# Logits of four of twelve token tiles by VectorE instead of TensorE, and a lighter sum of squares

## The chip, the cores and the metric

One core of one Trainium2 chip runs the whole program. The metric is device time in microseconds of one execution. TensorE's granted clock has two levels here, 2.4 GHz (written 1.00 in the profile) and 1.2 GHz (0.50).

## The reference, cut to what matters

Three layers follow one another on 1536 tokens (2 batches of 768) with 512 features:

```
attention: 16 heads, local window 96 and 8 global keys, softmax, times v     -> x
gated MLP: xn = x / sqrt(mean(x*x) + 1e-6) * rms_g
           x = (silu(xn @ w_gate) * (xn @ w_val)) @ w_out                    -> x
experts:   skip = x @ w_skip;  logits = x @ w_gate  (8 experts)
           tokens with skip > 0: e = argmax(logits), g = softmax(logits)[e]
           out = x + g * (relu(x @ w1[e]) @ w2[e]);  the others: out = x
```

## The kernel before, in words

The order of the work is written out by hand: each engine executes its instructions in the order in which the program issues them, and a wait of one instruction holds up everything behind it on the same engine.

**Attention** runs over 24 items (8 pairs of heads times 3 thirds of the sequence) in a pipeline of five steps, with `t` counting the turns. `Rms.take` leaves the square of each finished third in an `sq` tile, four of them to a batch. `Rms.add` (POOL, L422) adds one `sq` tile of 128x768 onto the first, at `t` = 3 pr + 8 for two head pairs of each batch, so that two tiles are left. `Rms.stats` then sums over the partitions by TensorE (L444): for each of 6 blocks of 128 tokens, one product per `sq` tile with a 128-column matrix of ones as moving operand; each fp32 product is two instructions in the trace. In its last call (`g == 3`) VectorE makes `rv` = mean + 1e-6 (L448). `Rms.root` takes the inverse square root in small VectorE steps. For batch 0 these are handed out one by one between VectorE's attention operations of later turns by `tick()`; for batch 1 they run in one go after the loop.

**The gated MLP** is two products. Every fp32 product is made of three (high x high, high x low, low x high). In the second one, `gemm2`, token tile `t` (128 tokens, 0 to 11) takes 36 matmuls, three to each of 12 steps `k`. A dictionary of hooks puts other work behind steps 1, 5 and 9 of a tile; the program there is, for tile `t`:

- ahead of step 0: `ranks(t-2)` (two small TensorE products from `cum` and `oh`), then VectorE's `select(t-2)` and `gates(t-2)` (eight small operations, from `rp` L707 to the last `val` L693);
- behind step 1 (`one`): `turn(t-1)`, four TensorE transposes of `x2` (L580) and a ScalarE copy to `x2t` (L581); `split_h(t+1)`, six ScalarE casts `hh` (L567) and six VectorE subtractions `hl` (L568), without which tile `t+1` cannot start;
- behind step 5 (`two`): `logits(t-1)`, eight TensorE instructions of 9 columns (L589); `route(t-1)`, seven small VectorE operations from `rm` (L653) over `oh` (L663) to `cum`; `exps(t-1)`, one on VectorE (L674) and an exponential on ScalarE (L677); in some tiles `split_next`, which splits chunks of 128x1024 of the experts' weights: `ewh` by ScalarE (L845), `ewl` by VectorE (L854);
- behind step 9: `slots(t-2)`, one TensorE product (L720) that reads what `gates` and `select` wrote;
- at the end ScalarE writes `x2` of tile `t` (L608).

`logits` and `ranks` share a ring of two PSUM buffers (tag `ps1`).

**The experts** follow. Their weights come through SP's DMA queue into `Slots`, a list of 128x1024 buffers; at the start of `gemm2` it holds 8, and 8 loads are issued (`load_next(8)`).

Of the kernel before, what the change touches and what calls it, by code (L numbers as in the profile page):

```python
# [191 lines left out]
def attention(s, rms):  # L192
# [8 lines left out]
    es = []  # L201
# [133 lines left out]
    for t in range(n + 4):  # L335
        a, b, c, d, e = (items[t - z] if 0 <= t - z < n else None for z in range(5))
        if a:
            qk(a, t)
        if c:
            trans(c, 0)  # L340
            trans(c, 1)
        if d:
            pv(d, 0)
            pv(d, 1)
        if b:
            zadd(b)
            tick()
            zrec(b)
            tick()
            norm(b, 1, 1, nc.gpsimd if t < n else nc.vector)  # L350
            if t < n:
                norm(b, 1, 0, nc.gpsimd)
            norm(b, 0, 0, nc.vector)
            tick()
        if a:
            ttr(a, 0, 0)
            tick()
        if b:
            norm(b, 0, 1, nc.vector)
            tick()  # L360
        if a:
            ttr(a, 0, 1)
            tick()
            ttr(a, 1, 0)
            tick()
        if b and t >= n:
            norm(b, 1, 0, nc.vector)
            tick()
        if a:
            ttr(a, 1, 1)  # L370
            tick()
        if c:
            evac(c, 0, nc.vector)
        if e:
            out(e)
        for half in range(2):
            if a:
                exp(a, half)
        if c:
            evac(c, 1, nc.scalar)  # L380
        if a:
            pr, g = a
            if g == 1 and 2 < pr + 2 < 8:
                load(pr + 2)
            if g == 2 and 2 < pr + 2 < 8:
                loadv(pr + 2)
        for pr in range(8):
            if pr % 4 in (1, 2) and t == 3 * pr + 8:
                rms[pr // 4].add()
        yield t  # L390


class Rms:
# [30 lines left out]
    def general(self, xg):  # L424

        s, nc = self.s, self.s.nc
        for hp in range(4):
            x = s.rpool.tile([128, 768], F32, name="gx", bufs=1)
            r = 512 * self.b + 128 * hp
            nc.sync.dma_start(x, xg[r:r + 128, :])  # L430
            sq = self.sq[hp] if hp < 2 else s.rpool.tile([128, 768], F32, name="gsq", bufs=1)
            for g in range(3):
                c = slice(256 * g, 256 * g + 256)
                self.parts(hp, g, x[:, c], sq[:, c])
            if hp > 1:
                nc.vector.tensor_tensor(self.sq[1], self.sq[1], sq, ALU.add)

    def stats(self, g, psum=None):
        s, nc = self.s, self.s.nc
        if g == 0:  # L440
            self.ss = psum or s.spare
        for j in range(2 * g, min(2 * g + 2, 6)):
            for z, sq in enumerate(self.sq):
                nc.tensor.matmul(self.ss[:, j:j + 128], lhsT=sq[:, 128 * j:128 * j + 128], rhs=s.ones,  # L444
                                 start=z == 0, stop=z == len(self.sq) - 1)
        if g == 3:
            self.v = s.rpool.tile([128, 6], F32, name="rv", bufs=2)
            nc.vector.tensor_scalar(self.v, self.ss[:, 0:6], 1.0 / 512.0, 1e-6, ALU.mult, ALU.add)  # L448

    def root(self):  # L450

        s, nc, v = self.s, self.s.nc, self.v
        r = s.r[self.b] = s.cpool.tile([128, 6], F32, name=f"r{self.b}")
        nc.vector.tensor_scalar(r.bitcast(I32), v.bitcast(I32), 1, None, ALU.arith_shift_right)
        yield
        nc.vector.tensor_scalar(r.bitcast(I32), r.bitcast(I32), -1.0, float(0x5F3759DF), ALU.mult, ALU.add)
        yield
        t = s.rpool.tile([128, 6], F32, name="rt", bufs=2)
        for _ in range(3):
            nc.vector.tensor_tensor(t, r, r, ALU.mult)  # L460
            yield
            nc.vector.scalar_tensor_tensor(out=t, in0=t, scalar=-0.5, in1=v, op0=ALU.mult, op1=ALU.mult)
            yield
            nc.vector.scalar_tensor_tensor(out=r, in0=t, scalar=1.5, in1=r, op0=ALU.add, op1=ALU.mult)
            yield
        d = self.diag = s.rpool.tile([128, 6, 128], F32, name="rd", tag="sq", bufs=4)
        for j in range(6):
            if j < 3:
                nc.vector.tensor_scalar(d[:, j, :], s.ident, r[:, j:j + 1], None, ALU.mult)
                yield  # L470
            else:
                nc.scalar.activation(d[:, j, :], s.ident, AF.Copy, scale=r[:, j:j + 1])
# [111 lines left out]
def logits(s, t, ks=range(4)):  # L584

    if ks[0] == 0:
        s.lg[t] = s.ps_g.tile([128, 9], F32, name="lg", tag="ps1", bufs=2)
    for k in ks:
        s.nc.tensor.matmul(s.lg[t], lhsT=s.xt[t][:, k, :], rhs=s.w9t[:, k, :], start=k == 0, stop=k == 3)  # L589


def gemm2(s, t, hooks={}):
# [103 lines left out]
def ranks(s, t, pool=None, tag="ps1"):  # L696

    rk = s.rk[t] = (pool or s.ps_g).tile([128, 8], F32, name="rk", tag=tag, bufs=1 if pool else 2)
    s.nc.tensor.matmul(rk, lhsT=s.ones16, rhs=s.cum[:, t, :], start=True, stop=False)
    s.nc.tensor.matmul(rk, lhsT=s.tri, rhs=s.oh[:, t, :], start=False, stop=True)  # L700


def select(s, t):

    V = s.nc.vector
    c = (s.ixpool if t >= 9 else s.hpool).tile([128, 8], F32, name="rp", bufs=2)
    V.tensor_tensor(c, s.oh[:, t, :], s.rk[t], ALU.mult)  # L707
    yield
    V.tensor_reduce(s.pos[:, t:t + 1], c, AX.X, ALU.add)
    yield  # L710
    sel = s.sel[t] = (s.ixpool if t >= 9 else s.hpool).tile([128, 256], F32R, name="sel", bufs=3 if t >= 9 else 2)
    V.tensor_scalar(sel, s.slot, s.pos[:, t:t + 1], None, ALU.is_equal)
    yield
# [10 lines left out]
def run(*parts):  # L724

    parts = list(parts)
    while parts:
        parts = [p for p in parts if next(p, FAR) is None]
# [213 lines left out]
def attn_moe_kernel(ctx, tc, qx, kx, vx, rel, ints, wgv, w_out, rms_g, w9, w9t, w1, w2, out):  # L942
# [96 lines left out]
    for t in att:  # L1039
        if t < 3:  # L1040
            next(bias)
        if t == 4:
            load_unit(s, units[0])
            load_unit(s, units[1])
        if t >= 13:
            next(unit, None)
        if t == 16:
            with tc.If(flag == 0):
                rms[0].general(s.xg)
        if t == 17:  # L1050
            for g in range(4):
                rms[0].stats(g)
            s.small = rms[0].root()
        if 19 <= t < 22:
            run(s.small)
            rms[0].spread(t - 19)
        if t in (25, 26, 27):
            gemm1s()
        if t == 26:
            ss = s.ps_n.tile([128, 133], F32, name="ss", tag="rb", bufs=2)  # L1060
            rms[1].stats(0, ss)
            rms[1].stats(1)
        if t == 27:
            rms[1].stats(2)
    with tc.If(flag == 0):
        rms[1].general(s.xg)
        for g in range(3):
            rms[1].stats(g, ss)
    rms[1].stats(3)


    run(rms[1].root())
# [57 lines left out]
        halves += [(j + 1, 0)] * (j < 8) + [(j, 1)]  # L1130
    loads = iter([(j, 4 * half + c) for j, half in halves for c in range(4)])
    s.slots = Slots()
    s.slots.add(rawpool, [f"raw{z}" for z in range(8)])

    def load_next(n, eng=nc.sync):
        for _ in range(n):
            x = next(loads, None)
            if x:
                if x == (8, 0):
                    experts[8].e = nc.values_load(  # L1140
                        s.eji[0:1, 0:1], engines=[mybir.EngineType.SP], min_val=0, max_val=7,
                        skip_runtime_bounds_check_because="a minimum with 7 of a count")
                experts[x[0]].load(x[1], eng)
# [8 lines left out]
            if x:  # L1152
                experts[x[0]].split(x[1], nc.scalar, nc.vector)

    load_next(8)
    s.early = s.ixpool.tile([128, 512], F32, name="early", bufs=1)
    nc.gpsimd.memset(s.early, 0.0)

    def routed(t):
        logits(s, t)  # L1160
        run(route(s, t))
        exps(s, t)

    for t in range(11):
        if t >= 2:
            ranks(s, t - 2)
            run(select(s, t - 2))
        if t >= 2:
            run(gates(s, t - 2))

        def one():
            if t >= 1:
                turn(s, t - 1)
                split_h(s, t + 1)
            if t in (2, 6, 10):
                for q in range(6):
                    s.slots.add(early if t < 10 and q == 0 else big, [f"h{t // 4}{q}"])
                load_next({6: 0, 10: 6}.get(t, 0))

        def two():  # L1180
            if t >= 1:
                routed(t - 1)
            split_next({2: 3, 3: 2, 6: 2, 7: 1}.get(t, 0))
            load_next({7: 4}.get(t, 0))

        gemm2(s, t, {(0, 1): one, (0, 5): two, (0, 9): lambda: t >= 2 and slots(s, t - 2)})


    slt = s.ixpool.tile([24, 256], F32, name="slt", bufs=1)
# [241 lines left out]
```

## Time and profile before

| | |
|---|---|
| median of 3 runs | 554.51 us (551.69 to 555.45) |
| profiled execution | 554.08 us, its span 552.3 us |
| TensorE (PE) busy | 524.2 us, 95% of the span |
| VectorE (DVE) | 404.8 us, 73% |
| ScalarE (ACT) | 277.5 us, 50% |
| GpSimd (POOL) | 140.8 us, 25% |

Times in the rows are microseconds from the start of the span. Attention takes the first 97 us or so, the gated MLP runs to about 423 us (`gemm2` from 303), the experts to the end. In a timeline, a row gives start, length, engine, line, operation, tile written <- tiles read, shapes and count; a bracket gives the idle time of the engine before it and who ended it.

### The profile page before, as it was taken

To read this page: it belongs to the slowest core of one execution; us is meant where nothing else is said; L and a number is where in the kernel's file an instruction comes from. 1 tells how busy PE (TensorE), PEld (TensorE's weight loads), DVE (VectorE), ACT (ScalarE), POOL (GpSimd) and SP (SyncE) were. 2 spreads that over 40 slices of the span, in tenths; PEclk is the share of its full clock that TensorE was granted. 3 is DMA by queue.
4 is the path that set the end of the run, shared out by engine and by line. 5 is a ranking of instruction groups with operands and counts; after the bars stand their busy time and mean duration, and the time that the engine had idled before them with its cause. 6 is when DMAs were issued, how large, how long until landed. Compare 5 with 4: busy or idle time off the path is not lost. (4 is left out here: it accounts for less than half of the span.)

```text
span 552.3 us, 9096 instructions
## 1 busy us (share of the span) xinstructions
PE 524.2 (95%) x3132; PEld 425.8 (77%) x3132; DVE 404.8 (73%) x1026; ACT 277.5 (50%) x631; POOL 140.8 (25%) x140
## 2 busy tenths in 40 slices
PE   3899886999999999999999999999999999999994
PEld 2676665878888888888888888878789787888883
DVE  5899999567888688868884358456443599999971
ACT  2799896324332233333333255244231587988850
POOL 2446545001222212212220200000000512666001
PEclk9999998999999999999999999999999999999998
DMA  8653511112323323323313512116171599999300
GB/s 301 210 211 139 173 36 39 33 46 77 105 88 113 113 79 114 114 79 113 115 38 130 214 39 78 39 52 215 39 293 57 202 393 395 398 399 396 131 15 16
DMA packets 28997, 80.62 MB, mean 146 GB/s; under 512 B 3512, under 2 KB 3768, under 8 KB 28945
## 3 DMA queue, kind: packets, MB, share of 16 engines
q1 hardware_dynamic: 24400, 68.61, 35.0%
q0 software_dynamic: 2672, 8.22, 3.9%
q10 hardware_dynamic: 1872, 3.15, 1.6%
q8 instruction: 26, 0.43, 0.3%
q14 instruction: 27, 0.21, 0.1%
HBM read 72.28 MB, written 8.65 MB: 147 GB/s over the span
## 5 line engine op out<-in xcount | busy, mean ns | idle before, releaser
L538 PE MATMUL ps<-xh,wh 128*128 128x512 f32 (+1 forms) x304 | 115.4, 380 | 0.1
L538 PE MATMUL ps<-xh,wl 128*128 128x512 f32 (+1 forms) x304 | 115.0, 378 | 0.5 <-POOL wl L504 0.5
L538 PE MATMUL ps<-xl,wh 128*128 128x512 f32 (+1 forms) x304 | 114.9, 378 | 0.0
L854 DVE TENSOR_TENSOR ewl<-eraw,ewh 128x1024 fp32r<-128x1024 f32 x72 | 83.5, 1220 | 6.2 <-ACT ewh L845 5.9
L845 ACT CAST ewh<-eraw 128x1024 fp32r<-128x1024 f32 x72 | 71.3, 1055 | 6.2 <-DVE ewl L854 4.2
L538 PEld LDWEIGHTS ps<-xh,wl 128*128 128x128 f32 x304 | 57.2, 188 | 11.6 <-POOL wl L504 0.9
L491 DVE SCALAR_TENSOR_TENSOR wraw<-f64t,wraw 128x512 f32<-128x512 f32 x36 | 44.7, 1241 | 28.8 <-ACT f64t L489 28.8
L538 PEld LDWEIGHTS ps<-xh,wh 128*128 128x128 f32 x304 | 57.2, 188 | 11.0 <-issue 0.7
L538 PEld LDWEIGHTS ps<-xl,wh 128*128 128x128 f32 x304 | 57.2, 188 | 10.6
L604 PE MATMUL px<-woh,hh 128*128 128x512 f32 (+1 forms) x156 | 61.8, 396 | 0.0
L604 PE MATMUL px<-woh,hl 128*128 128x512 f32 (+1 forms) x156 | 58.7, 376 | 0.0
L604 PE MATMUL px<-wol,hh 128*128 128x512 f32 (+1 forms) x156 | 58.2, 373 | 0.0
L504 POOL TENSOR_TENSOR wl<-f64t,wh 128x512 fp32r<-128x512 f32 x24 | 31.0, 1293 | 101.3 <-ACT wh L503 55.7
L503 ACT CAST wh<-f64t 128x512 fp32r<-128x512 f32 x24 | 14.9, 622 | 71.4 <-DVE f64t L501 68.1
L262 ACT ACTIVATE es<-es,m 128x192 f32<-128x192 f32 (+1 forms) x96 | 41.4, 434 | 11.5 <-DVE m L251 10.3
L278 POOL TENSOR_SCALAR es<-es,z 128x192 f32<-128x192 f32 x46 | 36.0, 791 | 36.2 <-ACT pts L297 11.7
L286 PE MATMUL pt<-ident,es 128*128 128x128 f32 x176 | 30.5, 305 | 10.1 <-DVE pts L295 6.6
L286 PEld LDWEIGHTS pt<-ident,es 128*128 128x128 f32 x176 | 20.7, 152 | 21.6 <-DVE pts L295 10.0
L568 DVE TENSOR_TENSOR hl<-h,hh 128x256 fp32r<-128x256 f32 x72 | 25.4, 422 | 15.8 <-ACT hh L567 15.8
L604 PEld LDWEIGHTS px<-woh,hl 128*128 128x128 f32 x156 | 29.3, 188 | 5.8
L604 PEld LDWEIGHTS px<-woh,hh 128*128 128x128 f32 x156 | 29.4, 188 | 4.9
L604 PEld LDWEIGHTS px<-wol,hh 128*128 128x128 f32 x156 | 29.5, 189 | 4.0
(195 smaller groups left out, 979.7 us busy)
## 6 DMA issues: line engine op xcount, KB each, us to landing
eraw<-in_w_dram SPq DMA_DIRECT2D x64, 512.0 KB, 11.2
wraw<-in_wgv_dram SPq DMA_DIRECT2D x24, 512.0 KB, 3.8
wraw<-in_w_out_dram SPq DMA_DIRECT2D x12, 512.0 KB, 3.5
vp<-in_vx_dram SPq DMA_DIRECT2D x8, 704.0 KB, 4.0
eraw<-in_w_dram POOLq DMA_DIRECT2D x8, 512.0 KB, 13.6
kd<-in_kx_dram SPq DMA_DIRECT2D x7, 464.0 KB
xm<-x SPq DMA_DIRECT2D x12, 256.0 KB
out_dram<-x ACTq DMA_DIRECT2D x12, 256.0 KB, 2.8
```

What stands on the lines that cost most here:

```text
L262: nc.scalar.activation(e[:, r, x, e0:e0 + n], e[:, r, x, e0:e0 + n], AF.Exp, bias=m[:, j:j + 1], scale=-1.0, accum_out=z[:, j:j + 1])
L278: eng.tensor_scalar(e[:, r, x, e0:e0 + n], e[:, r, x, e0:e0 + n], z[:, j:j + 1], None, ALU.mult)
L286: nc.tensor.transpose(pt[:, kt, x, :], e[:, r, x, 128 * kt:128 * kt + 128], s.ident)
L491: nc.vector.scalar_tensor_tensor(out=a.bitcast(F32), in0=t, scalar=F64_LEAST, in1=a.bitcast(F32), op0=ALU.is_ge, op1=ALU.mult)
L503: nc.scalar.copy(hi, t)
L504: eng.tensor_tensor(lo, t, f(hi), ALU.subtract)
L538: nc.tensor.matmul(p, lhsT=w[:, k, :], rhs=x[c][:, k, a:b], start=n == 0, stop=n == 11)
L568: nc.vector.tensor_tensor(hl[:, i, :], src, f(hh[:, i, :]), ALU.subtract)
L604: nc.tensor.matmul(p, lhsT=h[:, k, :], rhs=w[k][:, c:c + N], start=n == 0, stop=n == 35)
L845: eng.copy(wh, raw)
L854: eng.tensor_tensor(wl, raw, f(wh), ALU.subtract)
```

## The change

Four edits.

1. For the token tiles 1, 3, 5 and 7 (`rows`) `turn` and `logits` go. `row_logits` takes their place: nine VectorE instructions of 512 elements each, product of `x2` with one row of `w9` and the sum over the row, five of them in the tile after (behind `split_h`) and four in the one after that (again behind `split_h`). `route` and `exps` of such a tile come behind step 5 two tiles later, ahead of `route` of the tile between; `ranks`, `select` and `gates` behind step 9; `slots` behind step 1 of the next tile.
2. The rows of `w9` are spread over the partitions by five DMAs into five of the eight first `Slots` buffers, ahead of the three loads that remain there. These five become weight buffers in tile 9. Loads and splits of chunks are dealt out anew; 8 splits and 18 loads by the end of tile 10, as before.
3. The addition of head pair 6 goes, so batch 1 has three `sq` tiles. The products of `stats` write one column instead of 128.
4. The making of `rv` becomes the first step of `root`.

```diff
-            if pr % 4 in (1, 2) and t == 3 * pr + 8:
+            if pr in (1, 2, 5) and t == 3 * pr + 8:
                 rms[pr // 4].add()
...
-                nc.tensor.matmul(self.ss[:, j:j + 128], lhsT=sq[:, 128 * j:128 * j + 128], rhs=s.ones,
+                nc.tensor.matmul(self.ss[:, j:j + 1], lhsT=sq[:, 128 * j:128 * j + 128], rhs=s.ones[:, 0:1],
                                  start=z == 0, stop=z == len(self.sq) - 1)
-        if g == 3:
-            self.v = s.rpool.tile([128, 6], F32, name="rv", bufs=2)
-            nc.vector.tensor_scalar(self.v, self.ss[:, 0:6], 1.0 / 512.0, 1e-6, ALU.mult, ALU.add)
 
     def root(self):
...
+        v = s.rpool.tile([128, 6], F32, name="rv", bufs=2)
+        nc.vector.tensor_scalar(v, self.ss[:, 0:6], 1.0 / 512.0, 1e-6, ALU.mult, ALU.add)
+        yield
...
+def row_logits(s, t, es):
+
+    if es[0] == 0:
+        s.lg[t] = s.hpool.tile([128, 9], F32, name="lgd", bufs=1)
+    for e in es:
+        s.nc.vector.tensor_tensor_reduce(
+            out=s.w9b[4][:, 512:1024], in0=s.x2[t], in1=s.w9b[e // 2][:, 512 * (e % 2):512 * (e % 2) + 512],
+            scale=1.0, scalar=0.0, op0=ALU.mult, op1=ALU.add, accum_out=s.lg[t][:, e:e + 1])
...
-    s.slots.add(rawpool, [f"raw{z}" for z in range(8)])
+    s.slots.add(rawpool, [f"raw{z}" for z in range(3)])
+    s.w9b = [rawpool.tile([128, 1024], F32, name=f"w9b{z}", bufs=1) for z in range(5)]
+    for z in range(5):
+        rows = w9[2 * z:min(2 * z + 2, 9), :].rearrange("(o e) n -> o (e n)", o=1)
+        nc.sync.dma_start(s.w9b[z][:, 0:rows.shape[1]], rows.to_broadcast([128, rows.shape[1]]))
...
+    rows = (1, 3, 5, 7)
...
     for t in range(11):
-        if t >= 2:
-            ranks(s, t - 2)
-            run(select(s, t - 2))
-        if t >= 2:
-            run(gates(s, t - 2))
+        if t >= 2 and t - 2 not in rows:
+            ranked(t - 2)
 
         def one():
+            if t - 3 in rows:
+                slots(s, t - 3)
             if t >= 1:
-                turn(s, t - 1)
+                if t - 1 not in rows:
+                    turn(s, t - 1)
                 split_h(s, t + 1)
+            if t - 1 in rows:
+                row_logits(s, t - 1, range(5))
+            if t - 2 in rows:
+                row_logits(s, t - 2, range(5, 9))
...
         def two():
-            if t >= 1:
+            if t - 2 in rows:
+                run(route(s, t - 2))
+                exps(s, t - 2)
+            if t >= 1 and t - 1 not in rows:
                 routed(t - 1)
-            split_next({2: 3, 3: 2, 6: 2, 7: 1}.get(t, 0))
-            load_next({7: 4}.get(t, 0))
-
-        gemm2(s, t, {(0, 1): one, (0, 5): two, (0, 9): lambda: t >= 2 and slots(s, t - 2)})
+            if t == 9:
+                s.slots.add(rawpool, [f"w9b{z}" for z in range(5)])
+            split_next({2: 2, 3: 1, 6: 1, 7: 1, 8: 1, 9: 2}.get(t, 0))
+            load_next({2: 2, 3: 1, 6: 1, 7: 1, 8: 1, 9: 3}.get(t, 0))
+
+        def three():
+            if t - 2 in rows:
+                ranked(t - 2)
+            elif t >= 2:
+                slots(s, t - 2)
+
+        gemm2(s, t, {(0, 1): one, (0, 5): two, (0, 9): three})
```

`ranked(t)` runs `ranks`, `select` and `gates` of tile `t` in this order.

## Rows read from the trace of the kernel before

**Rows 1.** Windows: busy us (and instructions) per engine, granted clock, DMA share, GB/s.
```profile
84.00:97.00 13.00, 8.51 (x87) 6.66 (x86) 12.43 (x36) 8.48 (x28) 7.64 (x7) 0.81 0.12 42
...
303.00:412.00 109.00, 109.00 (x562) 89.07 (x562) 59.70 (x237) 45.51 (x115) 3.15 (x12) 1.00 0.32 118
```
**Rows 2.** Timeline of PE: tile 3 of `gemm2`, up to the start of tile 4.
```profile
330.95 0.18 PE L699 MATMUL rk<-cum,ones 128*128 128x8 bf16 x1
...
332.48 0.60 PE L580 MATMUL pxt<-ident,x 128*128 128x128 f32 x4
332.84 0.48 PE L604 MATMUL px<-woh,hh 128*128 128x512 f32 x1
333.15 0.39 PE L604 MATMUL px<-wol,hh 128*128 128x512 f32 x1
333.38 0.39 PE L604 MATMUL px<-woh,hl 128*128 128x512 f32 x1
...
335.68 0.96 PE L589 MATMUL lg<-w9t,x2t 128*128 128x9 f32 x8
336.49 0.47 PE L604 MATMUL px<-woh,hh 128*128 128x512 f32 x1
...
340.86 0.18 PE L699 MATMUL rk<-cum,ones 128*128 128x8 bf16 x1
```
**Rows 3.** Timeline of DVE: the end of tile 3, and tile 4.
```profile
339.39 2.54 DVE L854 TENSOR_TENSOR ewl<-eraw,ewh 128x1024 fp32r<-128x1024 f32 x2 [1.43 <-ACT ewh L845]
341.85 0.15 DVE L707 TENSOR_TENSOR rp<-oh,rk 128x8 f32<-128x8 bf16 x1
...
343.35 0.17 DVE L693 TENSOR_TENSOR val<-rg,val 128x8 fp32r<-128x8 f32 x1
343.95 2.10 DVE L568 TENSOR_TENSOR hl<-h,hh 128x256 fp32r<-128x256 f32 x6 [0.43 <-ACT hh L567]
346.58 0.17 DVE L653 TENSOR_REDUCE rm<-lg 128x1 f32<-128x8 f32 x1 [0.53 <-PE lg L589]
...
347.24 0.23 DVE L663 SCALAR_TENSOR_TENSOR oh<-rc,re,rdo 128x8 bf16<-128x8 f32 x1
...
347.72 0.15 DVE L674 TENSOR_SCALAR rm<-rm 128x1 f32<-128x1 f32 x1
```
**Rows 4.** Timeline of ACT: the exponential and the splits of tile 3.
```profile
338.05 0.27 ACT L677 ACTIVATE rex<-lg,rm 128x8 f32<-128x8 f32 x1 [2.51 <-DVE rm L674]
...
338.31 2.00 ACT L845 CAST ewh<-eraw 128x1024 fp32r<-128x1024 f32 x2
```
**Rows 5.** Groups by line and shape: count, busy us, mean ns, idle before and releaser.
```profile
L568 DVE TENSOR_TENSOR hl<-h,hh 128x256 fp32r<-128x256 f32 x72 | 25.4, 422 | 15.8 <-ACT hh L567 15.8
L251 DVE CUSTOM_DVE_ANT_0 es<-sc,bias 128x192 f32<-128x192 f32 x80 | 25.3, 351 | 1.1 <-PE sc L240 1.1
L498 DVE SCALAR_TENSOR_TENSOR f64t<-wraw,f64t 128x512 uint32<-128x512 uint32 x36 | 24.7, 691 | 1.0
...
L251 DVE CUSTOM_DVE_ANT_0 es<-sc,bias 128x64 f32<-128x64 f32 x8 | 1.7, 218 | 0.0
```
**Rows 6.** The page's part on DMA issues: count, KB each, us from issue to landing.
```profile
eraw<-in_w_dram SPq DMA_DIRECT2D x64, 512.0 KB, 11.2
```
**Rows 7.** Timelines around the end of attention, and a scaling of 192 columns earlier.
```profile
77.06 0.32 DVE L278 TENSOR_SCALAR es<-es,z 128x192 f32<-128x192 f32 x1
...
92.30 2.56 DVE L278 TENSOR_SCALAR es<-es,z 128x192 f32<-128x192 f32 x4
92.44 1.84 POOL L422 TENSOR_TENSOR sq<-sq 128x768 f32<-128x768 f32 x1 [0.42 <-ACT sq L415]
...
95.51 1.97 PE L286 MATMUL pt<-ident,es 128*128 128x128 f32 x8 [2.33 <-DVE pts L295]
```
**Rows 8.** Timeline at turn 17 of attention: sums of squares of batch 0.
```profile
65.38 2.94 PE L444 MATMUL po<-ones,sq 128*128 128x128 f32 x24
...
68.37 0.17 DVE L448 TENSOR_SCALAR rv<-po 128x6 f32<-128x6 f32 x1 [1.01 <-PE po L444]
```

More of the change, by code (lines that the diff above doesn't have):

```diff
@@ L430, in general @@
             nc.sync.dma_start(x, xg[r:r + 128, :])
-            sq = self.sq[hp] if hp < 2 else s.rpool.tile([128, 768], F32, name="gsq", bufs=1)
+            sq = self.sq[hp] if hp < len(self.sq) else s.rpool.tile([128, 768], F32, name="gsq", bufs=1)
             for g in range(3):
@@ L434, in general @@
                 self.parts(hp, g, x[:, c], sq[:, c])
-            if hp > 1:
-                nc.vector.tensor_tensor(self.sq[1], self.sq[1], sq, ALU.add)
+            if hp >= len(self.sq):
+                nc.vector.tensor_tensor(self.sq[-1], self.sq[-1], sq, ALU.add)
     def stats(self, g, psum=None):
@@ L443, in stats @@
             for z, sq in enumerate(self.sq):
-                nc.tensor.matmul(self.ss[:, j:j + 128], lhsT=sq[:, 128 * j:128 * j + 128], rhs=s.ones,
+                nc.tensor.matmul(self.ss[:, j:j + 1], lhsT=sq[:, 128 * j:128 * j + 128], rhs=s.ones[:, 0:1],
                                  start=z == 0, stop=z == len(self.sq) - 1)
-        if g == 3:
-            self.v = s.rpool.tile([128, 6], F32, name="rv", bufs=2)
-            nc.vector.tensor_scalar(self.v, self.ss[:, 0:6], 1.0 / 512.0, 1e-6, ALU.mult, ALU.add)
     def root(self):
-        s, nc, v = self.s, self.s.nc, self.v
+        s, nc = self.s, self.s.nc
+        v = s.rpool.tile([128, 6], F32, name="rv", bufs=2)
+        nc.vector.tensor_scalar(v, self.ss[:, 0:6], 1.0 / 512.0, 1e-6, ALU.mult, ALU.add)
+        yield
         r = s.r[self.b] = s.cpool.tile([128, 6], F32, name=f"r{self.b}")
@@ L1050, in attn_moe_kernel @@
         if t == 17:
-            for g in range(4):
+            for g in range(3):
                 rms[0].stats(g)
@@ L1068, in attn_moe_kernel @@
             rms[1].stats(g, ss)
-    rms[1].stats(3)
     run(rms[1].root())
@@ L1153, in split_next @@
                 experts[x[0]].split(x[1], nc.scalar, nc.vector)
-    load_next(8)
+    load_next(3)
     s.early = s.ixpool.tile([128, 512], F32, name="early", bufs=1)
@@ L1162, in routed, with ranked @@
         exps(s, t)
-    for t in range(11):
-        if t >= 2:
-            ranks(s, t - 2)
-            run(select(s, t - 2))
-        if t >= 2:
-            run(gates(s, t - 2))
+    rows = (1, 3, 5, 7)
+    def ranked(t):
+        ranks(s, t)
+        run(select(s, t))
+        run(gates(s, t))
+    for t in range(11):
+        if t >= 2 and t - 2 not in rows:
+            ranked(t - 2)
         def one():
+            if t - 3 in rows:
+                slots(s, t - 3)
             if t >= 1:
-                turn(s, t - 1)
+                if t - 1 not in rows:
+                    turn(s, t - 1)
                 split_h(s, t + 1)
+            if t - 1 in rows:
+                row_logits(s, t - 1, range(5))
+            if t - 2 in rows:
+                row_logits(s, t - 2, range(5, 9))
             if t in (2, 6, 10):
@@ L1177, in one @@
                     s.slots.add(early if t < 10 and q == 0 else big, [f"h{t // 4}{q}"])
-                load_next({6: 0, 10: 6}.get(t, 0))
+            if t == 10:
+                load_next(6)
         def two():
-            if t >= 1:
+            if t - 2 in rows:
+                run(route(s, t - 2))
+                exps(s, t - 2)
+            if t >= 1 and t - 1 not in rows:
                 routed(t - 1)
-            split_next({2: 3, 3: 2, 6: 2, 7: 1}.get(t, 0))
-            load_next({7: 4}.get(t, 0))
-        gemm2(s, t, {(0, 1): one, (0, 5): two, (0, 9): lambda: t >= 2 and slots(s, t - 2)})
+            if t == 9:
[8 more added lines that the diff above has]
+        gemm2(s, t, {(0, 1): one, (0, 5): two, (0, 9): three})
     slt = s.ixpool.tile([24, 256], F32, name="slt", bufs=1)
```

## Prediction

> **What bounds the kernel now.** I read the windows first. In the stretch that holds `gemm2` TensorE is busy for all of its 109 us, VectorE for 59.7 [rows 1]. So what leaves TensorE's stream there shortens the run, as long as nothing else comes late. The other row of this view is the end of attention: TensorE is busy 8.5 of 13 us, VectorE 12.4, and the granted clock is 0.81 in the mean. There VectorE sets the pace.
>
> Next I read TensorE's timeline through one tile, to see that it is packed: 9.91 us from one `ranks` to the next, and an undisturbed matmul every 0.23 us [rows 2]. Then I read VectorE and ScalarE against that tile [rows 3, 4], because the change hands them new work, and what counts is not how much idle time they have but what stands ahead of what in their queues.
>
> **The change, part by part.** I count in us from the start of a tile.
>
> *What TensorE loses.* A `turn` takes 332.84 - 332.48 = 0.36, and the matmul behind it is followed after 0.31 instead of 0.23: 0.44 in all. `logits` take 336.49 - 335.68 = 0.81 and, I assume, the same 0.08: 0.89 [rows 2]. Four tiles are spared both: 4 x 1.33 = **5.3 us less**. `ranks` and `slots` stay and only move.
>
> *What one product costs VectorE.* The trace has no product of 512 elements with a sum, but it has its relative in attention, on 64 and 192 elements: (351 - 218)/128 = 1.04 ns for an element, so 351 + 320 x 1.04 = 684 ns [rows 5]. Six `hl` of 422 ns take 2.10 us together, so each starts 0.34 after the one before, 0.08 ahead of its end [rows 3, 5]; with that overlap a product costs 0.60 us. All of them write the same scratch row; if each has to wait for the one before, it is 0.72 (0.684 and some 0.03). I take 0.60, since the relative's row is the nearest, and keep 0.72 for the range. 36 products are 21.7 us; VectorE has 49 idle us in that stretch [rows 1], but the queue decides.
>
> *The queue in an odd tile* (3, 5, 7, 9). `hl` ends at 343.95 + 2.10 - 340.86 = 5.2, as in tile 4 of the trace [rows 2, 3], because an odd tile still has its `turn` and ScalarE's copy ahead of the casts. The next operation can start at 5.1. Four products: 7.5. `route` of the tile in `rows`: its `oh` is ready 0.89 after its start [rows 3], at 8.4, just when TensorE comes to `ranks` behind step 9 (9.9 less two steps of three matmuls, 1.4). Then `route` of the even tile starts 1.2 later, at 8.7, and its last operation ends 1.29 after that, at 10.0. ScalarE's exponential waits for it; a chunk's `ewh` starts 0.26 behind the exponential, `ewl` 1.08 behind `ewh` [rows 3, 4]: 11.4. One `ewl` is 2.54/2 = 1.27: 12.6. Only behind it stand `select` and `gates` of the tile in `rows`, 343.35 + 0.17 - 341.85 = 1.67 [rows 3]: **14.3**.
>
> *Who waits for that.* `slots` of that tile is now behind step 1 of the next tile. TensorE gets there at 9.9 + 1.5 = 11.4 [rows 2] and stands until 14.3, with the whole tile queued behind: 2.9 us. Before, `slots` came behind step 9, at 8.5, and `gates` ended at 2.7 in tile 4 [rows 3], so the trace shows no such wait. Tile by tile: tile 3 splits one chunk, 2.9; tile 5 none, so `gates` end at 11.6; there `ranks` of the even tile is worse off, as its PSUM buffer is that of the `logits` whose exponential ends near 10.5: 0.6; tile 7 one chunk, 2.9; tile 9 two chunks, 2.9 + 1.3 = 4.2. Together **10.6 us more**. In even tiles VectorE is early: no `turn` ahead of the casts, so `hl` starts when `select` and `gates` end, near 1.9, and ends near 4.0, five products near 7.0, one `ewl` near 8.3, in a tile of 8.6; in tile 2 two chunks reach 0.9 into tile 3, where VectorE would wait for `hl` anyway. ScalarE's `x2` of tiles 3, 7 and 9 comes behind `ewh`, 1 to 2 us late; its readers stand behind the same waits, so I add nothing.
>
> The stage: 10.6 - 5.3 = **+5.3 us**; with 0.72 for a product each odd tile is 4 x 0.12 = 0.5 later, +7.2; with no wait at all, -5.3.
>
> *The addition of head pair 6.* While POOL adds, from 92.44 for 1.84 us, four VectorE scalings of `es` take 2.56; alone one takes 0.32, so four, with the overlap, some 1.04 [rows 7]. TensorE stands idle 2.33 behind them. Without the addition: **-1.5**, at least nothing, at most the 1.84 of POOL.
>
> *One-column sums.* A product of 9 columns costs 0.81/8 = 0.10 [rows 2], one of 128 columns 2.94/24 = 0.12 [rows 8]. 48 instructions at 0.12 become 60 at 0.10 (batch 1 now has three tiles): 6.0 - 5.8 = **+0.2**; if one column costs as much as 128, +1.4.
>
> *`rv` later.* VectorE stood 1.01 us for batch 0's sums [rows 8], with the scalings and score operations of the next turn behind it. Now it makes the next `z` first. From 0 (the wait comes one operation later) to -1.0; I take **-0.6**, as most of the sums' time is past by then. Batch 1's root runs in the same order as before: nothing.
>
> *DMAs.* Five spreads stand on SP ahead of three loads instead of eight. A 512 KB load lands 11.2 us after its issue [rows 6]; if they issue when `gemm2` starts, near 303, they land near 314, and the first product comes near 325. If the repeated rows read slower, this 11 us of cover is what they may use; beyond it VectorE would be late by the rest. Later loads wait on SP for `ewl` (12.6 in tile 3), and the store of `x2` stands behind; the first reader of those stores is in tile 11, so nothing. POOL's queue only gets shorter.
>
> **Sum.** +5.3 - 1.5 + 0.2 - 0.6 = +3.4. From the profiled execution, 554.08: 557.5. The median of the runs shown is 0.43 above that execution, which makes **558**. Own range of this case: 555.5 to 561, from the bounds of the product (+1.9), the sums (+1.2) and the attention terms (-0.7).
>
> **Rivals.** *VectorE comes in time* (faster). Mechanism: `gates` of the tiles in `rows` end before TensorE is 1.5 us into tiles 4, 8 and 10. For it: 49 idle us against 21.7 added. Against it: the order in the queue, by which they end 2.9 late; `ewl` would have to be free of the exponential, or the products be much cheaper. The point from which it decides is 11.4 us behind the start of the odd tile. Then -5.3 - 1.9 = 547.3. Chance 0.17; that about half of the waits come, 552 to 553, has 0.11.
>
> *The product runs at half rate* (slower). Two fp32 sources in SBUF and a sum at once is a form that this trace doesn't show: in the relative one source is in PSUM. For a plain operation with two such sources the row speaks against it: 691 ns for 512 elements [rows 5]. At twice 1.04 ns an element a product costs 1.13, each odd tile is 4 x 0.53 = 2.1 later, +8.5: 566. Chance 0.10. The Trainium skill (Vector Engine (DVE) Microarchitecture Reference, section 7, Points that are easy to get wrong) says that the two-source scalar form with two non-bf16 sources in SBUF runs at half throughput. The 691 ns row, which is such a form without a sum, does not bear this out, so I keep the chance low; by that rule the time would be this rival's.
>
> *TensorE's clock falls in the new waits* (slower). In the window at the end of attention 4.5 idle us in 13 went with a mean clock of 0.81, so 0.38 x 13 = 4.9 us at 1.2 GHz [rows 1]; at half speed that loses up to 2.5. Three waits of 2.9 to 4.2 would cost up to 7.4: 565. Against it: each is one gap in an otherwise packed stream. Chance 0.10.
>
> **How the numbers follow.** The forecast has 0.52, the likeliest, so 558. Range: 546.5 takes in the case in time, 563 the bounds of the forecast and half-grown cases of the clock; left out are the two slow rivals, 0.2. What can be told from no change is about 1%, 549.0 to 560.1. Faster: 0.17. Slower: the two slow rivals and a quarter of the forecast, 0.10 + 0.10 + 0.13 = 0.33. Same: 0.50.
>
> **What would show it.** In the profile after: products of 0.69 us, 0.60 apart; in tiles 4, 8 and 10 TensorE idle some 3, 3 and 4 us ahead of `slots` (L720), ended by VectorE's `val` (L693); even tiles else near 8.6 us; in tile 6 a short wait at `ranks`; the four scalings near 1.0 us and TensorE's transposes 1.5 earlier. I am wrong if `slots` doesn't wait, if VectorE runs its queue in another order than I read, if `ewl` of tiles 3, 7 and 9 starts before 10, or if a product is far from 0.69.

## The result, and the profile after

The changed kernel takes 560.11 us (median of 4 runs, 558.13 to 562.79) against 553.1 for the kernel before beside it: a ratio of 1.011, interval 1.008 to 1.014. The two medians are 7.0 us apart, 1.3%, which lies within the interval; the ratios here are the recorded ones, so they can differ a little from the quotient of two medians. It is a small loss; 558 us was forecast. The profiled execution took 561.94 us, with a span of 560.2 (before: 554.08 and 552.3).

In `gemm2` the lines of the kernel after stand 10 further down: `slots`' matmul is L730, `ranks` L709 and L710, `val` L703, `ewh` L855, `ewl` L864. The products are L597. In the rows `rk` is what `ranks` writes, `sl` what `slots` writes, `rex` the output of ScalarE's exponential.

First the windows of the kernel after, the same two stretches as in [rows 1] (the columns are those of that group, PE, PEld, DVE, ACT, POOL).

```profile
84.00:97.00 13.00, 9.58 (x99) 7.57 (x99) 11.84 (x36) 8.93 (x28) 5.67 (x6) 0.88 0.12 42
303.00:412.00 109.00, 99.02 (x469) 79.31 (x468) 79.74 (x292) 42.63 (x108) 3.15 (x12) 0.98 0.34 117
```

VectorE took over 20 us of work (59.7 to 79.7) and is still idle for 29. But TensorE, which was busy all 109 us, now lacks 10. The view of waits says where, for TensorE from 300 to 425 us (us in total, times, longest).

```profile
PE sl L730 <- DVE val L703: 7.4, 3, 3.2
PE rk L710 <- DVE oh L673: 1.4, 4, 0.4
PE rk L709 <- ACT rex L687: 1.1, 3, 0.4
```

The timeline of TensorE around the start of tile 4 shows all three in one place; it answers to [rows 2].

```profile
338.06 0.18 PE L709 MATMUL rk<-cum,ones 128*128 128x8 bf16 x1
338.64 0.17 PE L710 MATMUL rk<-oh,tri 128*128 128x8 bf16 x1 [0.40 <-DVE oh L673]
...
340.67 0.17 PE L709 MATMUL rk<-cum,ones 128*128 128x8 bf16 x1 [0.37 <-ACT rex L687]
...
344.46 0.29 PE L730 MATMUL sl<-sel,val 128*24 128x256 f32 x1 [2.10 <-DVE val L703]
```

VectorE's timeline over tile 3 (it starts near 329.87) is the queue of the prediction, read off; it answers to [rows 3].

```profile
332.87 2.10 DVE L568 TENSOR_TENSOR hl<-h,hh 128x256 fp32r<-128x256 f32 x6 [1.69 <-ACT hh L567]
334.89 0.69 DVE L597 CUSTOM_DVE_ANT_0 w9b<-x,w9b 128x512 f32<-128x512 f32 x1
335.50 0.09 DVE L597 DVE_READ_ACCUMULATOR2_ANT lgd<- 128x1 f32 x1
335.62 0.69 DVE L597 CUSTOM_DVE_ANT_0 w9b<-x,w9b 128x512 f32<-128x512 f32 x1
...
337.09 0.69 DVE L597 CUSTOM_DVE_ANT_0 w9b<-x,w9b 128x512 f32<-128x512 f32 x1
...
338.36 0.23 DVE L673 SCALAR_TENSOR_TENSOR oh<-rc,re,rdo 128x8 bf16<-128x8 f32 x1
...
340.02 0.15 DVE L684 TENSOR_SCALAR rm<-rm 128x1 f32<-128x1 f32 x1
341.59 1.23 DVE L864 TENSOR_TENSOR ewl<-eraw,ewh 128x1024 fp32r<-128x1024 f32 x1 [1.42 <-ACT ewh L855]
342.73 0.15 DVE L717 TENSOR_TENSOR rp<-oh,rk 128x8 f32<-128x8 bf16 x1
...
344.24 0.17 DVE L703 TENSOR_TENSOR val<-rg,val 128x8 fp32r<-128x8 f32 x1
```

VectorE stands still for 1.42 us ahead of `ewl`, although `gates` (from `rp` to `val`) could run: they stand behind `ewl`, and `ewl` waits for `ewh`, which on ScalarE waits for the exponential of the even tile. ScalarE's rows answer to [rows 4].

```profile
340.26 0.27 ACT L687 ACTIVATE rex<-lg,rm 128x8 f32<-128x8 f32 x1 [0.85 <-DVE rm L684]
...
340.52 1.04 ACT L855 CAST ewh<-eraw 128x1024 fp32r<-128x1024 f32 x1
```

Attention's end, VectorE's scalings and TensorE's transposes behind them, answers to [rows 7]; the sums of batch 0 and `rv` to [rows 8].

```profile
92.17 1.01 DVE L278 TENSOR_SCALAR es<-es,z 128x192 f32<-128x192 f32 x4
...
93.83 1.95 PE L286 MATMUL pt<-ident,es 128*128 128x128 f32 x8 [1.26 <-DVE pts L295]
...
65.12 2.84 PE L444 MATMUL po<-ones,sq 128*128 128x1 f32 x24
...
68.00 0.16 DVE L451 TENSOR_SCALAR rv<-po 128x6 f32<-128x6 f32 x1 [0.83 <-PE po L444]
```

Against the kernel before, TensorE's place was 0.12 us ahead at 83 us, and is 1.68 ahead at the transposes. At `gemm2`'s first matmul it is 0.42 *behind* (303.70 against 303.28). So attention gained and lost again, and `gemm2` lost the rest. From tile 11 on nothing differs (142.3 us to the end of the span, 142.1 before).

### The profile page after: what moved, and what is told of

Its sections match the earlier page's. It is cut to its first block, busy times and chain, and to the rows that moved or that the text cites. A ratio compares the mean times of both kernels' runs of the same rounds, so it can differ in the third digit from the quotient of the medians.

```text
span 560.2 us, 9105 instructions
## 1 busy us (share of the span) xinstructions
PE 522.8 (93%) x3096; PEld 423.5 (76%) x3096; DVE 426.9 (76%) x1098; ACT 275.5 (49%) x627; POOL 138.4 (25%) x139
## 5 line engine op out<-in xcount | busy, mean ns | idle before, releaser
L864 DVE TENSOR_TENSOR ewl<-eraw,ewh 128x1024 fp32r<-128x1024 f32 x72 | 83.7, 1232 | 4.6 <-ACT ewh L855 4.4
L855 ACT CAST ewh<-eraw 128x1024 fp32r<-128x1024 f32 x72 | 71.5, 1054 | 6.5 <-DVE ewl L864 4.3
## 6 DMA issues: line engine op xcount, KB each, us to landing
eraw<-in_w_dram SPq DMA_DIRECT2D x64, 512.0 KB, 11.4
```

What stands on the lines that cost most here:

```text
L855: eng.copy(wh, raw)
L864: eng.tensor_tensor(wl, raw, f(wh), ALU.subtract)
```

## The experiments

Two theories for `gemm2`. *Queue*: `slots` waits since `gates` stand behind `ewl` and the products on VectorE. *Clock*: the waits matter less than the half clock behind them, or behind the one-column sums. Nearly all experiments edit the kernel after; where another kernel is the base, it is said.

**Gates ahead of `ewl`.** In odd tiles the splits and loads (`dealt`, the lines of `two` that deal out splits and loads) run behind `ranked`, which is in `three`.

```
-            split_next({2: 2, 3: 1, ...}.get(t, 0))
-            load_next({2: 2, 3: 1, ...}.get(t, 0))
+            if t - 2 not in rows:
+                dealt(t)
             if t - 2 in rows:
                 ranked(t - 2)
+                dealt(t)
```

> Only the place of the splits and loads of chunks in tiles 3, 5, 7 and 9 is changed: behind select and gates of the tile in rows, no longer ahead of them. Queue theory (TensorE waits for slots because gates stand behind ewl): the waits of 2.10, 2.10 and 3.23 us ahead of slots in tiles 4, 8 and 10 go to under 0.5 each, the waits at ranks (0.3 to 0.4 each, eight at most) stay, and the half-speed stretch behind tile 10's wait goes: 7.4 + 1.5 less, so 551 to 552.5. Rival (VectorE has too much work per pair of tiles, whatever the order): the chunks now split later, so the wait moves to split_h or ranks of the next tile, and the time stays within 2 us of 560.

Measured: 551.84 us (7 runs), ratio to before 0.994 (0.991 to 0.997). TensorE's waits that are left:

```profile
PE rk L710 <- DVE oh L673: 1.4, 4, 0.4
PE pxt L580 <- ACT x L618: 1.0, 1, 1.0
```

The row of `slots` is gone, and 8 us with it. Not one product was taken from VectorE: the order of its queue made the loss.

**Products first as well.** To the edit before, this adds: in odd tiles the four products run ahead of `split_h`'s casts, in the time in which VectorE waited for ScalarE's `hh` (1.69 above).

```
+                if t - 2 in rows:
+                    row_logits(s, t - 2, range(5, 9))
                 split_h(s, t + 1)
             ...
-            if t - 2 in rows:
-                row_logits(s, t - 2, range(5, 9))
```

> As the kernel with gates ahead of the splits; besides, in tiles 3, 5, 7 and 9 the four products come ahead of split_h, where VectorE stood 1.7 to 2.9 us waiting for ScalarE's casts. Queue theory: route of the tile in rows starts 2 to 3 us earlier, so the waits at ranks go as well (3 us), gemm2 takes some 5 us less than in the kernel before, and the time is 547 to 550. Rival (too much work): no gain over the other order, 551 or more, with split_h late and step 0 of the next tile waiting for hl.

Measured: 548.44 us (4 runs), ratio 0.987 (0.983 to 0.992). No wait of TensorE is left in `gemm2`. The medians of the two kernels are 3.4 us apart; in the profiles tiles 2 to 10 of `gemm2` take 3.8 less (83.27 us against 87.10). These are the waits at `oh` and `pxt`, 2.4 in the view above, and what a stop costs beside its idle time: from `rk` L709 behind step 9 of an odd tile to that of the next tile it is 2.23 us with the wait of 0.39, 1.52 without.

**Products first alone**, with splits and gates where the change has them.

> The kernel after, with the four products of an odd tile ahead of its casts hl, where VectorE waits 1.69 us for ScalarE; splits and loads stay where the change has them (gates behind ewl). Theory (the queue on VectorE decides): some 1.7 us of the four products lie in that wait, gates end 1.7 earlier, the waits of slots shrink from 2.1, 2.1 and 3.2 to some 0.4, 0.4 and 1.5, the wait of ranks for oh goes, together 6 us less: 554. Rival (only the place of gates behind ewl decides, since ewl waits for ScalarE's ewh and not for VectorE's own queue): slots' waits stay above 1.5 each, 558 to 560.

Measured: 552.78 us (10 runs), ratio 0.999 (0.997 to 1.002). First what is left of TensorE's waits, then the timeline of VectorE up to tile 3:

```profile
PE sl L730 <- DVE val L703: 4.2, 3, 2.4
```

```profile
328.11 2.36 DVE L864 TENSOR_TENSOR ewl<-eraw,ewh 128x1024 fp32r<-128x1024 f32 x2
330.38 0.69 DVE L597 CUSTOM_DVE_ANT_0 w9b<-x,w9b 128x512 f32<-128x512 f32 x1
...
333.19 2.10 DVE L568 TENSOR_TENSOR hl<-h,hh 128x256 fp32r<-128x256 f32 x6
```

The time went below the 554 of the queue theory; the waits are a miss in size: 0.4, 0.4 and 1.5 were expected, 1.41, 0.34 and 2.43 came. In tile 3 the first product can start only when the two `ewl` of tile 2 end, at 330.4, 1.2 us into the tile; I had counted on VectorE being free. In tile 9 it is the same with the one `ewl` of tile 8, which holds up the first product until 1.1 us behind the tile's start at 386.18:

```profile
386.12 1.22 DVE L864 TENSOR_TENSOR ewl<-eraw,ewh 128x1024 fp32r<-128x1024 f32 x1
387.25 0.69 DVE L597 CUSTOM_DVE_ANT_0 w9b<-x,w9b 128x512 f32<-128x512 f32 x1
```

So the waits of tiles 4 and 10 shrank by 0.7 and 0.8 only. In tile 7 the first product starts as the tile does (367.36 and 367.38), and the wait came out as expected. By the medians either reordering alone wins back 7 to 8 us, both together 12.

**Two scratch rows.** Products came 0.735 us apart, not 0.60. Here those of odd rows of `w9` write their unused result to `early`, which is cleared later for that.

```
-            out=s.w9b[4][:, 512:1024], in0=...
+            out=s.early if e % 2 else s.w9b[4][:, 512:1024], in0=...
```

> The kernel after, but the products of odd rows of w9 write their unused result to a second scratch row (s.early, cleared later for that), so no product writes where the one before it wrote. In the kernel after products start 0.735 us apart, 0.04 after the end of the one before. Theory that they wait for each other's scratch row: 0.61 apart (0.08 ahead of the end of the one before, as hl's casts), four products 0.4 to 0.5 shorter in each odd tile, waits of slots 7.4 -> 6.0, time 558.5. Rival (the spacing belongs to the product itself, say to its sum): 0.735 apart as before, waits 7.4, time 560.

Measured: 562.13 us (4 runs), ratio 1.013 (1.007 to 1.020). VectorE's timeline of tile 3, then TensorE's waits:

```profile
334.90 0.69 DVE L597 CUSTOM_DVE_ANT_0 early<-x,w9b 128x512 f32<-128x512 f32 x1
335.51 0.09 DVE L597 DVE_READ_ACCUMULATOR2_ANT lgd<- 128x1 f32 x1
335.51 0.69 DVE L597 CUSTOM_DVE_ANT_0 w9b<-x,w9b 128x512 f32<-128x512 f32 x1
...
336.12 0.69 DVE L597 CUSTOM_DVE_ANT_0 early<-x,w9b 128x512 f32<-128x512 f32 x1
```

```profile
PE sl L730 <- DVE val L703: 7.5, 3, 3.2
PE rk L709 <- ACT rex L687: 1.1, 3, 0.4
```

The spacing is the shared scratch row's: 0.61 with two. But the expectation on `slots` failed, and what failed in it is instructive. The wait at `oh` went (1.4); that at `slots` stayed, since in this order both its ends hang on the same exponential. `ranks` of the even tile waits for `rex` (its PSUM buffer), and `slots` comes 1.5 us of matmuls later; `ewh`, `ewl` and `gates` start from `rex` too. Products that end earlier move both. And the waits had a price of their own here. Behind each of the three, TensorE's granted clock fell to half; windows behind the first:

```profile
344.00:345.00 1.00, 0.90 (x5) 1.00 0.42 147
345.00:346.00 1.00, 1.00 (x5) 0.63 0.92 367
346.00:347.00 1.00, 1.00 (x4) 0.50 0.60 223
347.00:348.00 1.00, 1.00 (x3) 0.50 0.00 0
348.00:349.00 1.00, 1.00 (x4) 0.66 0.00 0
```

(Columns: PE's busy us, granted clock, DMA share, GB/s.) From `slots` of this tile to the next `slots` it is 7.22 us, and 5.62 in the kernel after, where the clock held: **1.6 us for one fall**. With two falls more than the kernel after this outweighs the 1.5 us that the spacing gave: from tile 2 to tile 11 it is 98.31 us, and 96.51 in the kernel after.

**128 columns in the kernel after** (`rhs=s.ones`, as before the change).

> The changed kernel with products of 128 columns in the sums of squares again (still three tiles of squares in batch 1). Clock theory (24 one-column products in a row let TensorE's granted clock fall, seen from 111 to 115 us): no half-speed stretch behind the sums, clock 1.00 from 98 us to gemm2, gemm2 starts 1 to 2 us earlier, time 558 to 559. Rival (the clock fell because of the idle gaps at 88 to 94 us, or by chance): the stretch stays or comes in some runs, and the time is 560 to 561, since 60 products cost 0.02 us more each.

Measured: 563.47 us (4 runs), ratio 1.016 (1.011 to 1.020): not the 558 to 559 of the clock theory. TensorE's waits are the same as in the kernel after (7.5, 1.4, 1.1). `gemm2` doesn't start 1 to 2 us earlier (303.87 against 303.70): in this execution TensorE came to the sums of batch 1 1.7 us later (108.91 against 107.24), in part as its clock stood at half from 93 to 99 us, and from 94 to 97 in the kernel after. The clock held behind the sums, but fell behind two of `slots`' waits, where it fell behind one in the kernel after:

```profile
344.00:345.00 1.00, 0.37 (x3) 1.00 0.75 131
345.00:346.00 1.00, 1.00 (x5) 0.74 0.83 250
346.00:347.00 1.00, 1.00 (x4) 0.50 0.95 373
```

**Sums alone** (the kernel before, with the addition, `rv` and one-column sums only), and **the addition alone** (the same, sums 128 columns wide).

```
-            if pr % 4 in (1, 2) and t == 3 * pr + 8:
+            if pr in (1, 2, 5) and t == 3 * pr + 8:
```

> The kernel before with the sums of squares changed alone (one addition fewer, one column, rv as root's first step), logits all by TensorE. If the addition's 1.5 us is a gain and the half-speed stretch takes it back, gemm2 starts within 0.5 us of the kernel before and the time is 552.5 to 554. If the stretch behind the sums doesn't come in this kernel: 551 to 552. If the sums alone were part of the loss: 555 or more.

> The kernel before with only the addition of head pair 6 and rv's place changed (three tiles of squares in batch 1, rv first in root); the sums stay 128 columns wide, gemm2 as before. By the prediction's terms: -1.5 (addition), -0.6 (rv), +12 products of 0.12 = +1.4: 0.7 less, 553.2 against a before of 553.9. Theory from the kernel after (the 1.5 is real, rv's place gives nothing, the twelve products take it back): 553.8, no difference; no stretch at half clock at 67 to 75 or 109 to 117 us, since no sums of one column. Rival (the addition's 1.5 is not taken back): 552.4 or less.

Measured: 554.76 us (10 runs), ratio 1.000 (0.997 to 1.002), and 553.22 (11 runs), ratio 0.998 (0.997 to 0.999). The sums alone bring no gain, where 552.5 to 554 was expected: `gemm2` starts 0.8 us later than in the kernel before (304.10 against 303.28). The addition alone, with the twelve products more and `rv`, is worth 0.6 to 1.7 us, so the products don't take its gain back whole, as the theory there had it; that the column makes the difference between the two isn't shown, as the intervals touch. The rows of the addition alone repeat those of the kernel after: four scalings in 1.01 us at 91.43, transposes at 93.09 instead of 95.51, of which 0.86 was there at 83 us (82.67 against 83.53), which leaves 1.56.

**Logits alone, well placed.** The kernel before, with the logits of four tiles on VectorE and both reorderings; attention untouched.

> The kernel before with only the logits of four tiles on VectorE, placed so that nothing waits (gates ahead of ewl in odd tiles, products ahead of hl); attention and its sums as before. Theory (four tiles are spared 1.33 each on TensorE and every wait is gone): 5.3 less than before, 548.6. Rival (TensorE loses more by a turn and logits than the timeline shows, or less): 1 us or more away from that; tile starts tell it, tile 2 to tile 11 should take 83.8 against 89.1.

Measured: 549.24 us (4 runs) against 554.59: ratio 0.990 (0.988 to 0.991), 5.4 us less by the medians and 5.8 by the ratio. In the same window as at the top TensorE is busy throughout again; then, from its timeline, the starts of tiles 2 and 11:

```profile
303.00:412.00 109.00, 109.00 (x557) 89.44 (x556) 83.28 (x317) 45.62 (x115) 4.42 (x13) 1.00 0.42 151
```

```profile
322.28 0.18 PE L709 MATMUL rk<-cum,ones 128*128 128x8 bf16 x1
...
405.55 0.18 PE L709 MATMUL rk<-cum,ones 128*128 128x8 bf16 x1
```

They are 83.27 us apart, against 89.14 before (321.04 to 410.18): 5.87 for four tiles, 1.47 each.

**Width of the sums in the well placed kernel.** The first time 128 columns took 546.49 us (ratio 0.989, 0.984 to 0.993), so both were run once more beside each other.

> The kernel with gates ahead of ewl and products ahead of hl (548.4), with the sums of squares 128 columns wide again instead of one. Theory that the one-column sums bring the stretches at half clock behind them (67 to 75 and 111 to 116 us): those stretches go, sums of batch 0 and 1 cost the same to 0.5 us, 545.5 to 547. Rival (the width of the sums changes nothing that counts; stretches at half speed come where TensorE idles): 548 to 549.

> The well placed kernel with one-column sums once more (548.4 the first time), beside the next one on the same chip, to weigh the width of the sums with more runs. Theory (one-column sums bring half clock behind them): 1 to 3 us above the next. Rival: the same to 0.5 us.

> The well placed kernel with sums 128 columns wide (546.5 the first time), beside the one before. Theory: 1 to 3 us below it, 545.5 to 547, and faster than both kernels of the study. Rival: the same to 0.5 us.

Measured: one column 547.94 us (6 runs; 0.987, 0.985 to 0.990), 128 columns 547.06 (4 runs; 0.986, 0.984 to 0.987). 0.9 us with overlapping intervals: not told apart. The clock behind the sums does differ in the profiles. Windows with one column, then, of the other kernel, with 128:

```profile
65.00:75.00 10.00, 10.00 (x85) 0.66 0.42 128
```

```profile
65.00:75.00 10.00, 9.70 (x117) 1.00 0.39 128
```

In the seven profiles with one-column sums the clock fell behind them, at 67 to 75 or 109 to 117 us, in every one; in the six with 128 columns (the kernel before among them) in none.

The kernel with 128 columns has the lowest medians of the study: by its last ratio it is 1.4% faster than before, and by the two ratios to before 2.5% faster than the change.

## Why the prediction was right

It forecast 558 us by a queue, and the queue is what happened: the edit that takes `gates` out from behind `ewl` removes the waits at `slots`. Of the size, part is luck. Term by term, as starts of tiles give it, from tile 2 to tile 11 (96.51 us after, 89.14 before: +7.4; +5.3 was forecast):

| term | predicted | measured |
|---|---|---|
| turn and logits of four tiles | -5.3 | -5.9 (logits alone, well placed) |
| tile 4: waits | +2.9 | +3.4: 1.09 more between the `rk`s, 2.28 more from `rk` to `slots` |
| tile 6 | +0.6 | +0.6 |
| tile 8 | +2.9 | +3.3 |
| tile 10 | +4.2 | +4.4 |
| half clock behind tile 10's wait | 0 | +1.5 |

The waits are measured against the well placed kernel, where 1.52 us lie between the two `rk` and 1.51 from `rk` to `slots`. Together they come to +11.8, and the table's sum is +7.4, of which the queue and the spared work make +5.9.

*The path.* `val` was forecast at 14.3 us into the odd tile; it ended 14.5 in (344.41 - 329.87). `ewl`, forecast at 11.4, started at 11.7. What I took for one wait of 2.9 at `slots` is split into three: 0.4 at `oh`, 0.37 at `rex`, 2.10 at `slots`. I had `oh` ready just as TensorE comes to it, at 8.4; it came 0.3 late, as products were 0.735 apart, and TensorE was there 0.3 sooner than I counted (8.2 us into the tile).

*The product.* Its duration was right, 691 ns (684 from the relative); the overlap I took was wrong. The upper bound, 0.72, was the right reading, for the reason given with it: the shared scratch row. The stage with that bound was +7.2; that +7.4 lies near it is luck, since 1.5 of the 7.4 is the half clock, and four tiles spared 5.9 and not 5.3. The queue with the overlap I took came closer: with two scratch rows (0.61) the stop between the two `rk` is 0.37 shorter in each odd tile, so the waits would be 11.8 - 1.5 = 10.3, and 10.6 was forecast. The rival at half rate is dead: 36 products of 691 ns. The rule named with it, from the Trainium skill (Vector Engine (DVE) Microarchitecture Reference, section 7, Points that are easy to get wrong), is one of the two-source scalar form; this product, with two fp32 sources in SBUF and a sum, doesn't show half throughput at 691 ns either.

*In time*, the rival on the fast side, failed by its own point of decision (`gates` before 11.4). The experiments show that its idea was sound: VectorE has room for 36 products, if `ewl` is not ahead of `gates`.

*The clock rival* was half right. One wait of three cost 1.5 us in the profiled execution, two and three in the kernels with 128 columns and two scratch rows. It is 1.5 to 1.6 a fall, not the up to 2.5 that the rival took for each wait, and it doesn't come each time. Whether that is why the runs of the change lie 4.7 us apart isn't shown: those of the kernel before, which has no such waits, lie 3.8 apart.

*Attention.* The addition: -1.5 forecast, -1.56 measured (1.68 less the 0.12 from earlier). The sums: +0.2 forecast, but one column costs 0.118 us (2.84/24), not 0.10, so 60 of them take 7.0 us against 5.9 for 48 of 128 columns: +1.1. `rv`: -0.6 forecast; its wait went from 1.01 to 0.83, since only the next `z` (0.16) is done ahead of it: -0.2. Together -0.7 instead of -1.9, and in the profiled execution a stretch of half clock behind batch 1's first 24 one-column products took that back too. It cost 1.5 us: eight matmuls from 110.83 on take 3.29 us, eight at full clock in the kernel before 1.82. The kernel before has a stop of its own there, the last row, which costs it 0.6 and which the kernel after doesn't have; so -0.7 + 1.5 - 0.6 = +0.2 of the +0.42 at `gemm2`'s start is accounted for.

```profile
110.00:111.00 1.00, 1.00 (x5) 0.98 0.02 8
111.00:112.00 1.00, 1.00 (x4) 0.50 0.26 33
...
114.00:115.00 1.00, 1.00 (x5) 0.82 0.03 12
...
114.49 0.50 PE L538 MATMUL ps<-xh,wl 128*128 128x512 f32 x1 [0.45 <-POOL wl L504]
```

*The sum.* In the profiled executions the change costs +7.9 (561.94 - 554.08), where +3.4 was forecast: `gemm2` came 2.1 worse, attention 2.3 (+0.4 instead of -1.9). Both misses go the same way. By the medians it is +7.0 against +3.5; the time itself came 2.1 above the forecast, as the kernel before ran 1.4 below the median that the sum was referred to (553.1, 554.51). On the median that the sum was referred to, +7.0 would have been 561.5, above the case's own range; that 560.11 lies inside it is luck. That range was too narrow for its own terms: its lower end, 555.5, doesn't follow from the -0.7 named for it (558 - 0.7 = 557.3), and it left out that the addition and `rv` might bring nothing (+2.1) and any half clock. Of my three chances the middle one was the largest; 1.1% (0.8 to 1.4) lies at its bound of 1%, and the runs don't tell on which side.

## What to carry to other kernels

Idle time on an engine that takes over work is not room: ask what the moved work, and the consumers moved with it, stand behind in that engine's queue, and whether the head of the queue waits for a third engine. If a result that the bottleneck needs stands behind a long operation that nobody is waiting for, swap the two; here that swap alone was worth 8 us, and both reorderings turned a loss of 1.1% into a gain of 1.3%. When you shorten a step, check whether the wait's two ends hang on the same event: then the wait stays as it is.

## What the runs showed that I had not expected

- Products with a sum that write one scratch row run 0.735 us apart; with two rows in turn 0.61, the next one starting with the read of the sum before it.
- Behind a wait of 2.1 to 3.2 us in an otherwise packed stream TensorE's granted clock fell to 0.50 in 6 of 9 cases (three kernels, three waits each), at a cost of 1.5 to 1.6 us; in the well placed kernels, without these waits, and with waits of 0.34 to 2.43 in the one with products first alone, in none.
- The clock fell behind one-column fp32 products although the busy rows of TensorE are full (10.00 of 10.00 us above), and not behind products of 128 columns.
- One column costs 0.118 us, 128 columns 0.123 (2.94/24): the width buys next to nothing. From the first of 24 to the matmul behind them it is 2.59 us at either width (107.24 to 109.83 in the kernel after, 106.50 to 109.09 in the addition alone).
